# Hash-masked attention with a fused MLP: the first weight pieces loaded in another order, and a new written-out order of all instructions

## The chip, the cores and the metric

The kernel runs on one core of a Trainium2 chip. The metric is the device time of one execution in microseconds (us), taken as the median of a few runs. Beside these runs, one execution was recorded by the hardware profiler; all durations below come from that record.

A core has a matrix engine (PE, with its weight loads PEld), a vector engine (DVE), an activation engine (ACT), a general engine (POOL) and a synchronising engine (SP). Each executes its own queue strictly in the order in which it was given. Transfers are issued by SP, ACT or POOL and carried out by 16 DMA engines.

## The reference

The inputs are `q`, `k`, `v` of shape (4 batches, 8 heads, 768 positions, 64), a projection of 64 by 6, a scale of 512, and two MLP weights of 512 by 2048 and 2048 by 512, all float32.

```
bits   = (x @ proj) > 0                    # 6 bits for each row of q and of k
mask   = bucket(q bits) == bucket(k bits)
scores = where(mask, q @ k.T / 8, -1e9)
attn   = softmax(scores) @ v               # per batch and head
x      = heads side by side                # (4, 768, 512)
xn     = (x - mean) / sqrt(var + 1e-6) * g_ln
out    = x + relu(xn @ w_ch1) @ w_ch2
```

## The kernel before

**Units and stages.** The output rows are cut into 12 units of 256 rows; unit `u` belongs to batch `u // 3`. A unit has two head groups `g` of four heads, and three key pieces `kp` of 256 keys, so attention is 72 steps `s`, with `u = s // 6`, `g = (s % 6) // 3`, `kp = s % 3`. The mask is not a select: the bits of q and k, as plus or minus one half, are multiplied on PE into the same PSUM accumulation as the scores, so that a mismatch makes the exponent very small.

**The steps by name.** The order text calls the steps by short words, `name.engine.arguments`, where the engine letter is `t` for PE, `v` for DVE, `a` for ACT, `p` for POOL and `s` for SP. Those that matter below:

| word | engine | what it does | line |
|---|---|---|---|
| `lx`, `LX.b.g.t` | SP (one on ACT) | load q (`t`=0) or k (`t`=1) of a head group, of batch 0 in pieces, of later batches whole | L373, L508 |
| `lv.b.hs.c` | SP | load v of four heads; batch 0 whole, later ones in four pieces | L465, L467 |
| `lw1.p.n`, `lw2.p.n` | POOL | load quarter `n` of the first or second MLP weight, float32 in HBM to bf16 in SBUF | L446, L457 |
| `tn`, `tu` | DVE | transpose 32 by 32 blocks of q or k, batch 0 and later batches | L304 |
| `ca`, `CA` | DVE, ACT or POOL | cast the transposed q or k to bf16, batch 0 and later ones | L311 to L315 |
| `ha`, `hc`, `sl`, `hm` | PE | projections for the bits (float32), in several layouts | L394, L405, L418, L526 |
| `bh`, `bc`, `bt`, `bi` | DVE (`bi` also ACT) | turn projections into bits, or copy them | L307, L428, L430 |
| `mw`, `mr` | SP | write the bits to DRAM, and read them back in the layout of PE | L544, L547 |
| `cv`, `su`, `sp`, `sq`, `sc` | several | v to bf16, and its sums | L473 to L502 |
| `S`, `E`, `A` | PE, ACT, PE | scores of a step, their exponent, product with v | L570, L576, L595 |
| `na`, `nb`, `nc`, `ag`, `rs`, `ce` | DVE (`rs` POOL) | normalise the attention, statistics, centre and scale the row | L608 to L636 |
| `ft`+`fc`, or `fl` | PE+ACT/DVE, or SP | transpose the row; unit 0 on PE, later units by a DMA transpose | L644, L648, L650, L639 |
| `wg.v.n` | DVE | multiply quarter `n` of the first weight by the scale | L454 |
| `F`, `R` | PE, ACT or DVE | first MLP product of a unit in eight pairs of columns, and its relu | L657, L665, L667 |
| `D`, `Z` | PE, DVE | second product of unit 0, and its addition | L672, L675 |
| `sw`, `ss`, `P`, `Y` | DVE, DVE, PE, DVE | second product of units 1 to 11 by seven products instead of eight | L697, L708, L723, L728 |
| `O` | SP or ACT | store the output | L740, L742 |

**What sets the order.** The order is written out. `ORDER` is a text of 1185 words that a loop runs through, and every engine gets its part of the instructions in just that sequence. A step that waits holds back all that stands behind it in the same queue, on SP and POOL too. The buffers are written out as well: `SLOTS` says for each buffer pool which buffer each new tile takes.

```
    with tc.manual_schedule():
        for word in ORDER.split():
            name, eng, *args = word.split(".")
            OPS[name](ENGINES[eng], *map(int, args))
```

A later load of q or k reuses the buffer of an earlier one. Before the four loads of batch 1, POOL writes one element into the buffer (`gx`, L505), which waits until the transposes have read the old contents. SP's transfers take turns on eight semaphores: a transfer is issued only when the eighth one before it has landed.

**The start.** Nothing can run on PE until q and k of batch 0 have come in pieces, been transposed on DVE, projected and turned into bits. Then steps 0 to 5 run, and with them the attention of unit 0, while DVE transposes q and k of batch 1. Unit 0's first MLP product `F.0.3` needs the row of unit 0 and the weight quarter 1, scaled by `wg.v.1`. From there on attention steps and MLP products of earlier units alternate on PE until the end.

Of the kernel before, what the change touches and what calls it, by code (L numbers as in the profile page):

```python
# [22 lines left out]
E.a.1.1 bh.v.1.0.0 E.a.2.0 tn.v.0.0.1 ha.t.1.1.0 A.t.1.2 ca.p.1.1.0 sq.t.0.0 A.t.0.2 E.a.2.1
ca.v.1.0.0 S.t.4.2 bh.v.1.1.0 E.a.4.0 E.a.4.1 tn.v.1.1.2 sc.v.0.0 A.t.2.2 ca.p.1.1.2 ca.v.0.0.1
na.v.0.0 ha.t.1.1.2 bh.v.1.1.2 S.t.3.2 nb.v.0.0 E.a.3.1 E.a.3.0 hc.t.0.0.1 bc.v.0.0.1 tn.v.1.0.1
gx.p.1.0.1 sl.t.0.0.1 cv.p.0.4.2 tn.v.1.0.2 S.t.5.2 E.a.5.0 cv.v.0.4.0 E.a.5.1 bi.v.0.0.1 gx.p.1.1.0
hc.t.1.0.1 lw1.p.3 lg.s LX.s.1.0.0 tu.v.1.0.0.3 tu.v.1.0.0.2 S.t.8.2 E.a.8.1 sq.t.0.4 LX.s.1.0.1
E.a.8.0 bc.v.1.0.1 sl.t.1.0.1 A.t.4.2 lw1.p.1 tu.v.1.0.0.0 tn.v.0.0.2 lw1.p.2 tu.v.1.0.1.3 sc.v.0.4
A.t.5.2 lw1.p.0 tu.v.1.0.1.2 A.t.3.2 na.v.0.1 lw2.p.0 bi.a.1.0.1 S.t.6.2 tu.v.1.0.0.1 hc.t.1.0.2
bc.v.1.0.2 lw2.p.3 ca.a.1.0.1 nc.v.0.0 gx.p.1.1.1 LX.s.1.1.1 E.a.6.0 hc.t.0.0.2 E.a.6.1 bc.v.0.0.2  # L30
lv.s.1.4.1 sl.t.1.0.2 lv.s.1.4.2 lw2.p.2 S.t.7.2 E.a.7.1 sl.t.0.0.2 nb.v.0.1 lv.s.1.4.0 bi.v.0.0.2
bi.v.1.0.2 gt.t tu.v.1.0.1.1 tu.v.1.0.1.0 nc.v.0.1 ag.v.0.0 ag.v.0.1 S.t.9.2 E.a.7.0 E.a.9.1
gc.v ce.v.0.1 LX.s.1.1.0 hm.t.1.0 lv.s.1.0.0 lv.s.1.0.1 S.t.10.2 ce.v.0.0 ft.t.0.0 bt.v.1.0
ft.t.0.1 wg.v.1 mw.s.1.0 E.a.9.0 fc.v.0.1 A.t.6.2 lv.s.1.0.3 fc.a.0.0 lv.s.1.4.3 A.t.8.2
ca.a.0.0.2 A.t.7.2 wg.v.3 E.a.10.1 F.t.0.3 E.a.10.0 na.v.1.0 wg.v.2 S.t.11.2 E.a.11.0
R.v.0.3 F.t.0.4 R.v.0.4 nb.v.1.0 nc.v.1.0 F.t.0.7 E.a.11.1 S.t.14.2 lv.s.1.0.2 A.t.11.2
E.a.14.1 A.t.10.2 F.t.0.6 E.a.14.0 R.v.0.7 wg.v.0 A.t.9.2 CA.v.1.0.0 R.a.0.6 rs.p.0
S.t.12.2 mr.s.1.0.0 na.v.1.1 E.a.12.1 F.t.0.0 R.a.0.0 tu.v.1.1.0.3 F.t.0.1 R.v.0.1 mr.s.1.0.2
ca.v.1.0.2 mr.s.1.0.1 CA.p.1.0.1 E.a.12.0 nb.v.1.1 S.t.13.2 nc.v.1.1 ag.v.1.1 F.t.0.2 F.t.0.5
E.a.13.1 tu.v.1.1.1.0 R.a.0.2 S.t.16.2 D.t.0.0.0 E.a.13.0 A.t.13.2 ag.v.1.0 A.t.12.2 rs.p.1  # L40
tu.v.1.1.1.1 LX.s.2.0.1 tu.v.1.1.1.3 A.t.14.2 tu.v.1.1.0.0 tu.v.1.1.1.2 E.a.16.1 E.a.16.0 R.a.0.5 CA.a.1.1.1
na.v.2.0 D.t.0.0.1 tu.v.1.1.0.1 S.t.15.2 E.a.15.1 tu.v.1.1.0.2 hm.t.1.1 bt.v.1.1 S.t.17.2 D.t.0.1.0
E.a.15.0 D.t.0.1.1 nb.v.2.0 ce.v.1.0 A.t.16.2 mr.s.1.0.3 ce.v.1.1 A.t.15.2 E.a.17.0 E.a.17.1
A.t.17.2 su.p.1.0 cv.a.1.0.2 sw.v.3.1 na.v.2.1 nb.v.2.1 nc.v.2.1 CA.a.1.1.0 S.t.18.2 E.a.18.0
E.a.18.1 D.t.0.1.2 mw.s.1.1 D.t.0.1.3 Z.v.0.1 S.t.20.2 E.a.20.1 cv.v.1.0.0 fl.s.1.0 LX.s.2.0.0
E.a.20.0 nc.v.2.0 tu.v.2.0.0.2 D.t.0.0.2 D.t.0.0.3 S.t.19.2 Z.v.0.0 fl.s.1.1 ag.v.2.0 cv.a.1.4.0
ag.v.2.1 F.t.1.0 E.a.19.0 rs.p.2 tu.v.2.0.0.3 R.v.1.0 F.t.1.4 mr.s.1.1.0 A.t.18.2 tu.v.2.0.0.1
R.v.1.4 sw.v.2.1 sw.v.4.1 mr.s.1.1.2 ce.v.2.0 sw.v.3.0 F.t.1.2 sp.t.1.0 E.a.19.1 sw.v.2.0
mr.s.1.1.1 mr.s.1.1.3 S.t.21.2 sc.a.1.0 R.a.1.2 E.a.21.1 F.t.1.3 E.a.21.0 A.t.19.2 A.t.20.2
na.v.3.0 R.a.1.3 F.t.1.6 R.a.1.6 sw.v.4.0 S.t.22.2 LX.s.2.1.0 LX.s.3.0.1 sw.v.1.0 E.a.22.0  # L50
ce.v.2.1 fl.s.2.1 F.t.1.5 tu.v.2.0.0.0 R.v.1.5 E.a.22.1 F.t.1.7 nb.v.3.0 fl.s.2.0 R.a.1.7
S.t.23.2 E.a.23.1 P.t.1.2 Y.v.1.2 F.t.1.1 R.v.1.1 sw.v.1.1 S.t.24.2 E.a.23.0 lv.s.2.0.3
# [734 lines left out]
```

## Time and profile before

| | |
|---|---|
| median of 3 runs | 297.76 us (297.38 to 298.34) |
| the profiled execution, its own time | 298.12 us |
| its span, first to last instruction | 296.4 us |
| busy: PE, PEld | 286.4 us (97%), 227.6 us (77%) |
| busy: DVE, ACT, POOL | 210.8 us (71%), 202.9 us (68%), 57.1 us (19%) |
| mean granted PE clock | 0.993 |
| chain that ended last | PE 83%, DVE 7%, DMA 4%, issue 2% |
| transfers | 34.10 MB, mean 115 GB/s |

The profiled execution's time is 1.7 us longer than its span; that is work around the kernel. It lies 0.36 us above the median of the runs. PE is called busy in 97% of the span, but matmul ends are modelled and matmuls that wait in the middle of a group still count as busy, so the share hides stalls. They are found by the number of matmuls in a stretch, or by the time from one step's start to the next.

### The profile page before, as it was taken

The numbers are of one execution on the slowest core, as the hardware profiler recorded it, in microseconds if no ns is written. First come the engines' busy times: TensorE is split into PE (matmuls) and PEld (weight loads), VectorE is DVE, ScalarE is ACT, GpSimd is POOL, SyncE is SP. The second block draws the span as 40 slices with busy tenths as digits, with TensorE's granted clock in tenths as the row PEclk, the third lists the DMA queues.
The fourth block names the chain that finished last, engine by engine and source line by source line (L and its number), as shares of the span: only waits on it lengthen the run. The fifth ranks groups of instructions, "written<-read, shape, count | busy, mean of one in ns | idle before, by whom it ended". The sixth has DMA issues, their size and how long they took to land.

```text
span 296.4 us, 10520 instructions
## 1 busy us (share of the span) xinstructions
PE 286.4 (97%) x4646; PEld 227.6 (77%) x4650; DVE 210.8 (71%) x479; ACT 202.9 (68%) x227; POOL 57.1 (19%) x92
## 2 busy tenths in 40 slices
...
GB/s 216 313 336 159 278 291 240 162 160 222 38 189 65 201 157 13 216 115 2 30 102 143 63 154 29 55 62 2 73 39 2 71 22 2 108 0 108 0 91 72
DMA packets 31055, 34.10 MB, mean 115 GB/s; under 512 B 15521, under 2 KB 27809, under 8 KB 31010
## 3 DMA queue, kind: packets, MB, share of 16 engines
q1 hardware_dynamic: 25938, 28.72, 35.5%
...
## 4 chain that ended last, share of the span: by engine, by line
PE 83%; DVE 7%; DMA 4%; issue 2%; SPq 1%; ACT 1%; DVEq 0%; ACTq 0%
PE f L657 24%; PE sc L570 16%; PE X L723 12%; PE acc L595 10%; PE Yb L723 7%; PE Ya L723 3%; DMA xnT<-xc 3%; PE hf L394 3%; PE f L672 2%; PE hp L526 2%; ACT E L576 1%; DVE xc L630 1%; PE warm L363 1%; DMA out_dram<-x 1%; DVE hb L667 1%
## 5 line engine op out<-in xcount | busy, mean ns | idle before, releaser
L576 ACT ACTIVATE E<-sc,bias_sb 128x1024 bf16<-128x1024 f32 x144 | 153.3, 1112 | 44.8 <-PE sc L570 42.8
L657 PE MATMUL f<-xnT,w_sb 128*128 128x256 bf16 x768 | 93.4, 273 | 1.0 <-DMA xnT<-xc 1.0
L657 PEld LDWEIGHTS <-w_sb 128*128 128x128 bf16 x768 | 71.6, 98 | 14.0 <-issue 4.4
L665 ACT ACTIVATE hb<-f 128x512 bf16<-128x512 f32 x60 | 35.7, 596 | 32.5 <-PE f L657 32.4
L570 PE MATMUL sc<-qb,kb 32*128 32x256 bf16 x1152 | 53.1, 268 | 0.0
L570 PE MATMUL sc<-G 6*128 6x256 bf16 (+1 forms) x576 | 42.7, 273 | 1.3 <-DVE y L608 0.6
L595 PEld LDWEIGHTS <-E 128*128 128x128 bf16 x1152 | 40.7, 98 | 4.1 <-issue 2.5
L595 PE MATMUL acc<-vaug,E 128*128 128x65 bf16 x1152 | 43.5, 194 | 0.0
L723 PEld LDWEIGHTS <-hb 128*128 128x128 bf16 x352 | 32.9, 98 | 6.9 <-issue 3.1
L667 DVE TENSOR_SCALAR hb<-f 128x512 bf16<-128x512 f32 x36 | 24.5, 681 | 15.5 <-PE f L657 15.3
L635 POOL TENSOR_SCALAR rs<-mv 128x2 f32<-128x2 f32 x12 | 3.2, 270 | 160.5 <-DVE mv L624 155.5
L570 PEld LDWEIGHTS <-kb 32*128 32x128 bf16 x1152 | 30.8, 93 | 1.7
L728 DVE TENSOR_TENSOR x<-X,x 128x256 f32<-128x256 f32 x44 | 18.3, 418 | 18.5 <-PE X L723 18.2
L570 PEld LDWEIGHTS <-G 6*128 6x128 bf16 (+1 forms) x576 | 15.8, 91 | 17.3 <-issue 15.2
L723 PEld LDWEIGHTS <-S 128*128 128x128 bf16 x264 | 24.9, 97 | 4.7 <-issue 1.3
L304 DVE STREAM_TRANSPOSE T<-X 128x384 f32<-128x384 f32 (+2 forms) x52 | 26.6, 536 | 0.0
L723 PE MATMUL Yb<-w_sb,S 128*128 128x256 bf16 x176 | 22.9, 273 | 0.0
L723 PE MATMUL X<-wt,hb 128*128 128x256 bf16 x168 | 21.8, 273 | 0.0
L608 DVE SCALAR_TENSOR_TENSOR y<-vsB,acc 128x520 f32<-128x520 f32 x24 | 16.4, 685 | 6.4 <-PE acc L595 6.2
L617 DVE TENSOR_TENSOR x<-y,rc 128x512 f32<-128x512 f32 x24 | 16.6, 692 | 2.4 <-issue 1.2
L621 DVE BATCH_NORM_STATS2 st<-x 128x6 f32<-128x256 f32 x48 | 17.8, 414 | 0.3
L728 DVE TENSOR_TENSOR x<-Yb,x 128x256 f32<-128x256 f32 x22 | 9.2, 419 | 8.6 <-PE Yb L723 8.5
...
## 6 DMA issues: line engine op xcount, KB each, us to landing
...
w_sb<-in_moe_w_ch_dram POOLq DMA_DIRECT2D x8, 512.0 KB, 16.1
...
```

What stands on the lines that cost most here:

```text
L304: nc.vector.transpose(d[:, j], s[:, j, kj0 : kj0 + n])
L570: nc.tensor.matmul(sc(s, i // 2)[:, i % 2, 256 * kk : 256 * kk + 256], lh, rh, start=(rep == 0), stop=(rep == 2), skip_group_check=True,)
L576: nc.scalar.activation(E(s)[:, heads(h)], sc(s, h), AF.Exp, scale=EXP_SCALE, bias=bias_sb)
L595: nc.tensor.matmul(acc[:, qt, (D + 1) * i : (D + 1) * (i + 1)], E(s)[:, i, 256 * kk + P * qt : 256 * kk + P * qt + P], vaug(u // 3)[:, 4 * ...
L608: nc.vector.scalar_tensor_tensor(yt(u, g), vs, EPS_ROW, made[f"acc{u}{g}"][:, :, :A], op0=AOP.mult, op1=AOP.add,)
L617: nc.vector.tensor_tensor(xo, a[:, :, :, 0:D], rc.to_broadcast([P, 2, 4, D]), op=AOP.mult)
L621: nc.vector.bn_stats(stats(u)[:, qt, g], xt(u)[:, qt, 256 * g : 256 * g + 256])
L657: nc.tensor.matmul(f1[:, n].rearrange("p (t x) -> p t x", t=2), w1_sb[:, dt, P * nt : P * nt + P], xnT(u)[:, :, dt], start=(dt == 0), stop ...
L665: nc.scalar.activation(hb(u)[:, 2 * p : 2 * p + 2], f1, AF.Relu)
L667: eng.tensor_scalar_max(hb(u)[:, 2 * p : 2 * p + 2], f1, 0.0)
L723: nc.tensor.matmul(f2, lh[:, n], rh[:, n], start=(first and n == 0), stop=(n == 7), skip_group_check=True)
L728: nc.vector.tensor_tensor(x, made[f"{prod(u, k)}{u}"], x, op=AOP.add)
```

## The change

The diff rewrites `ORDER` and `SLOTS`, and nothing else. Its first lines and one of the buffer lines:

```diff
-mem.v lp.a lx.a.0.1.0.1 tab.a pf.v lx.s.0.0.0.1 warm.t wm.t.0 wm.t.1 wm.t.2
-wm.t.3 sel.p tn.v.0.0.0 p32.p tn.v.0.1.0 ca.p.0.1.0 lx.s.0.1.1.3 ha.t.0.0.0 wm.t.4 lx.s.1.1.0.3
+lp.a lx.a.0.1.0.1 lx.s.0.0.0.1 lx.s.0.1.1.3 lx.s.1.1.0.3 lx.s.1.0.0.1 lv.s.0.0.4 lx.s.0.0.1.3 lv.s.0.4.4 lx.s.1.0.1.3
+lg.s on.p.0 mem.v tab.a pf.v warm.t wm.t.0 wm.t.1 wm.t.2 wm.t.3
+sel.p tn.v.0.0.0 p32.p tn.v.0.1.0 on.p.1 lw1.p.3 ca.a.0.0.0 ha.t.0.1.0 wm.t.6 ha.t.0.0.0
...
-    X="0123023102132001",
+    X="0123021302312012",
```

 Both orders have the same 1185 steps. What differs is the sequence, the engine of some steps, and the buffers.

*The weights.* Before, the only weight piece among the first loads was quarter 1 of the second weight (`lw2.p.1`), and the other seven followed in one row. Now it is quarter 3 of the first weight (`lw1.p.3`), and the other three quarters of the first weight come next; the second weight's quarters stand further back. POOL's queue, all steps up to the last weight piece:

```
before: sel p32 ca.0.1.0 lw2.1 ca.0.1.1 ca.1.1.1 on.0 gx.1.0.0 pmem on.1 cv.0.0.2 cv.0.0.0 ca.1.1.0 ca.1.1.2 gx.1.0.1
        cv.0.4.2 gx.1.1.0 lw1.3 lw1.1 lw1.2 lw1.0 lw2.0 lw2.3 gx.1.1.1 lw2.2 rs.0 CA.1.0.1 rs.1 ...
after:  on.0 sel p32 on.1 lw1.3 ca.0.1.0 ca.0.1.1 ca.0.1.2 gx.1.0.0 cv.0.0.0 gx.1.0.1 ca.1.1.2 gx.1.1.1 cv.0.4.0 cv.0.4.2
        gx.1.1.0 lw1.1 lw1.2 lw1.0 pmem rs.0 lw2.1 lw2.0 CA.1.0.1 lw2.3 rs.1 lw2.2 ...
```

*SP's queue.* The first nine loads are unchanged. After them:

```
before: LX.1.0.0 LX.1.0.1 LX.1.1.1 lv.1.4.1 lv.1.4.2 lv.1.4.0 LX.1.1.0 lv.1.0.0 lv.1.0.1 mw.1.0 lv.1.0.3 lv.1.4.3 lv.1.0.2
        mr.1.0.0 mr.1.0.2 mr.1.0.1 LX.2.0.1 mr.1.0.3 mw.1.1 fl.1.0 LX.2.0.0 fl.1.1 mr.1.1.0 mr.1.1.2 mr.1.1.1 mr.1.1.3 ...
after:  LX.1.0.0 LX.1.0.1 mw.1.0 LX.1.1.0 mr.1.0.1 LX.1.1.1 lv.1.0.2 mr.1.0.2 lv.1.0.3 mr.1.0.3 mr.1.0.0 mw.1.1 lv.1.0.0
        lv.1.4.1 fl.1.1 lv.1.0.1 mr.1.1.2 mr.1.1.1 mr.1.1.0 fl.1.0 mr.1.1.3 lv.1.4.3 lv.1.4.2 LX.2.0.1 lv.1.4.0 ...
```

*DVE's queue in the start*, from the first transposes to the centred row of unit 0:

```
before: tn.0.0.0 tn.0.1.0 bh.0.0.0 tn.0.1.1 bh.0.1.0 tn.0.1.2 tn.1.1.1 bh.0.1.1 bh.1.1.1 tn.1.1.0 tn.1.0.0 bh.0.1.2 bh.1.0.0
        tn.0.0.1 ca.1.0.0 bh.1.1.0 tn.1.1.2 sc.0.0 ca.0.0.1 na.0.0 bh.1.1.2 nb.0.0 bc.0.0.1 tn.1.0.1 tn.1.0.2 cv.0.4.0 bi.0.0.1
        tu x2 bc.1.0.1 tu tn.0.0.2 tu sc.0.4 tu na.0.1 tu bc.1.0.2 nc.0.0 bc.0.0.2 nb.0.1 bi.0.0.2 bi.1.0.2 tu x2 nc.0.1 ag x2
        gc ce.0.1 ce.0.0
after:  tn.0.0.0 tn.0.1.0 bh.0.1.0 tn.0.1.1 bh.0.0.0 bh.0.1.1 tn.0.1.2 tn.1.1.0 bh.0.1.2 tn.1.1.1 tn.1.0.0 ca.1.1.0 bh.1.1.1
        ca.1.0.0 ca.1.1.1 bh.1.0.0 tn.1.1.2 cv.0.0.2 tn.0.0.2 bh.1.1.0 sc.0.0 tn.0.0.1 na.0.0 nb.0.0 bh.1.1.2 bc.0.0.1 tn.1.0.2
        bi.0.0.1 tn.1.0.1 sc.0.4 tu bc.1.0.2 tu x2 bc.1.0.1 tu x3 na.0.1 bc.0.0.2 nb.0.1 tu x2 nc.0.1 bi.0.0.2 nc.0.0 ag x2
        ce.0.0 ce.0.1 (gc follows)
```

*Engines.* Of the relus, 21 go from DVE to ACT and 17 the other way (64 on ACT instead of 60). Of the casts of q and k of later batches, ACT has 2 instead of 6, DVE 7 instead of 4, POOL 3 instead of 2. In the start, `ca.0.0.1`, `bi.1.0.2` and `fc.0.1` go from DVE to ACT, `ca.1.1.0` and `ca.1.1.1` from POOL to DVE, and `ca.0.1.2` from ACT to POOL.

*PE's queue.* From the first MLP product on, it holds the same groups at nearly the same places; for example, from unit 1's second product:

```
before: F.1.7 S.23 P.1.2 F.1.1 S.24 P.1.1 F.2.1 A.23 S.26 A.22 P.1.5 ...
after:  S.23 F.1.7 F.1.1 S.24 F.2.1 A.22 P.1.2 A.23 S.26 P.1.1 P.1.5 ...
```

More of the change, by code (lines that the diff above doesn't have):

```diff
@@ L23 @@
[L23 to L52, printed above, removed]
@@ new lines @@
+E.a.4.0 E.a.4.1 gx.p.1.0.1 tn.v.0.0.2 ca.a.0.0.2 bh.v.1.1.0 A.t.2.2 sq.t.0.0 LX.s.1.0.1 sc.v.0.0
+A.t.1.2 A.t.0.2 ca.p.1.1.2 tn.v.0.0.1 ca.a.0.0.1 gx.p.1.1.1 S.t.3.2 ha.t.1.1.2 E.a.3.0 cv.p.0.4.0
+na.v.0.0 hc.t.0.0.1 nb.v.0.0 E.a.3.1 bh.v.1.1.2 bc.v.0.0.1 S.t.5.2 E.a.5.1 sl.t.0.0.1 tn.v.1.0.2
+bi.v.0.0.1 cv.p.0.4.2 sq.t.0.4 tn.v.1.0.1 E.a.5.0 sc.v.0.4 hc.t.1.0.2 S.t.8.2 E.a.8.0 gx.p.1.1.0
+tu.v.1.0.0.2 bc.v.1.0.2 hc.t.1.0.1 lw1.p.1 tu.v.1.0.0.3 A.t.4.2 tu.v.1.0.0.0 A.t.3.2 E.a.8.1 bc.v.1.0.1
+lw1.p.2 sl.t.1.0.1 bi.a.1.0.1 A.t.5.2 tu.v.1.0.0.1 tu.v.1.0.1.2 lw1.p.0 sl.t.1.0.2 bi.a.1.0.2 ca.a.1.0.1
@@ new lines @@
+tu.v.1.0.1.0 S.t.6.2 E.a.6.0 E.a.6.1 na.v.0.1 hc.t.0.0.2 bc.v.0.0.2 sl.t.0.0.2 nb.v.0.1 tu.v.1.0.1.1
+tu.v.1.0.1.3 S.t.7.2 hm.t.1.0 E.a.7.0 S.t.9.2 nc.v.0.1 bi.v.0.0.2 nc.v.0.0 ag.v.0.0 ag.v.0.1
+ce.v.0.0 ce.v.0.1 pmem.p rs.p.0 gt.t E.a.7.1 A.t.7.2 A.t.6.2 A.t.8.2 bt.v.1.0
+gc.v E.a.9.0 E.a.9.1 ft.t.0.1 fc.a.0.1 wg.v.1 ft.t.0.0 fc.a.0.0 lw2.p.1 S.t.10.2
+E.a.10.0 E.a.10.1 na.v.1.0 F.t.0.3 wg.v.3 wg.v.2 R.a.0.3 S.t.11.2 F.t.0.7 E.a.11.0
+mw.s.1.0 F.t.0.4 R.v.0.7 LX.s.1.1.0 R.v.0.4 S.t.14.2 F.t.0.6 E.a.11.1 A.t.9.2 E.a.14.1
@@ new lines @@
+nb.v.1.0 nc.v.1.0 E.a.14.0 mr.s.1.0.1 A.t.11.2 A.t.10.2 wg.v.0 LX.s.1.1.1 lv.s.1.0.2 mr.s.1.0.2
+lw2.p.0 S.t.12.2 R.a.0.6 na.v.1.1 lv.s.1.0.3 nb.v.1.1 E.a.12.1 CA.p.1.0.1 tu.v.1.1.0.2 mr.s.1.0.3
+nc.v.1.1 CA.v.1.0.0 ag.v.1.0 E.a.12.0 F.t.0.1 R.a.0.1 F.t.0.0 S.t.13.2 ag.v.1.1 E.a.13.1
+E.a.13.0 lw2.p.3 mr.s.1.0.0 A.t.14.2 A.t.12.2 R.v.0.0 F.t.0.5 F.t.0.2 rs.p.1 tu.v.1.1.0.0
+tu.v.1.1.1.0 tu.v.1.1.0.1 ce.v.1.1 A.t.13.2 na.v.2.0 ca.a.1.0.2 nb.v.2.0 lw2.p.2 S.t.16.2 R.a.0.2
+R.a.0.5 E.a.16.1 D.t.0.0.0 D.t.0.0.1 tu.v.1.1.0.3 E.a.16.0 tu.v.1.1.1.3 tu.v.1.1.1.1 tu.v.1.1.1.2 CA.p.1.1.1
@@ new lines @@
+CA.a.2.1.0 F.t.3.1 R.v.3.1 mr.s.2.1.2 mr.s.2.1.1 E.a.38.0 F.t.3.3 R.v.3.3 mr.s.2.1.0 A.t.33.2
+na.v.5.1 E.a.38.1 tu.v.3.0.0.0 F.t.3.5 R.a.3.5 F.t.3.2 R.a.3.2 S.t.36.2 E.a.36.0 P.t.3.1
+ss.v.3.1 ss.v.3.2 P.t.3.2 Y.v.3.2 S.t.39.2 O.s.2.1 E.a.36.1 ss.v.3.4 P.t.3.5 E.a.39.0
+cv.p.2.0.2 A.t.36.2 LX.s.3.0.1 Y.v.3.1 P.t.3.6 Y.v.3.5 P.t.3.3 O.s.2.3 E.a.39.1 S.t.40.2
+E.a.40.0 E.a.40.1 ss.v.3.3 Y.v.3.6 Y.v.3.3 P.t.3.7 fl.s.4.0 nb.v.5.1 fl.s.4.1 tu.v.3.0.1.0
+F.t.4.3 Y.v.3.7 tu.v.3.0.0.2 P.t.3.4 Y.v.3.4 O.s.3.0 on.p.3 A.t.37.2 nc.v.5.1 ag.v.5.0
@@ new lines @@
+ag.v.7.0 P.t.5.5 E.a.52.0 mr.s.3.1.3 na.v.8.0 S.t.53.2 E.a.53.1 Y.v.5.5 P.t.5.3 Y.v.5.1
+nb.v.8.0 P.t.5.6 ss.v.5.3 mr.s.3.0.1 E.a.53.0 Y.v.5.6 mr.s.3.1.0 Y.v.5.3 S.t.54.2 CA.v.3.1.0
+P.t.5.7 E.a.54.0 F.t.6.0 R.a.6.0 A.t.53.2 Y.v.5.7 ag.v.7.1 P.t.5.4 E.a.54.1 rs.p.7
+F.t.6.6 Y.v.5.4 O.s.5.1 O.s.5.2 F.t.6.3 R.a.6.3 S.t.55.2 mr.s.3.1.2 R.v.6.6 A.t.52.2
+A.t.51.2 na.v.8.1 E.a.55.1 E.a.55.0 F.t.6.4 ce.v.7.0 S.t.56.2 R.a.6.4 ce.v.7.1 su.p.3.0
+F.t.6.5 E.a.56.1 F.t.6.2 R.a.6.5 E.a.56.0 S.t.58.2 R.v.6.2 E.a.58.1 fl.s.7.0 P.t.6.2
@@ new lines @@
+nc.v.8.0 Y.v.6.2 ss.v.6.1 ss.v.6.2 P.t.6.1 E.a.58.0 Y.v.6.1 cv.p.3.0.2 A.t.56.2 nb.v.8.1
+ss.v.6.3 sp.t.3.0 sc.a.3.0 nc.v.8.1 A.t.55.2 S.t.57.2 E.a.57.1 fl.s.7.1 F.t.7.5 R.a.7.5
+A.t.54.2 cv.a.3.4.0 na.v.9.0 P.t.6.6 Y.v.6.6 ss.v.6.4 E.a.57.0 P.t.6.5 Y.v.6.5 ag.v.8.0
+S.t.59.2 P.t.6.7 ag.v.8.1 Y.v.6.7 P.t.6.3 Y.v.6.3 rs.p.8 E.a.59.0 E.a.59.1 S.t.60.2
+E.a.60.1 E.a.60.0 O.s.5.3 F.t.7.0 O.s.5.0 cv.p.3.4.2 A.t.58.2 P.t.6.4 Y.v.6.4 R.a.7.0
+A.t.57.2 S.t.61.2 E.a.61.0 O.s.6.1 E.a.61.1 su.p.3.4 sp.t.3.4 ce.v.8.1 fl.s.8.1 ce.v.8.0
@@ new lines @@
+sc.v.3.4 F.t.7.4 F.t.7.6 R.a.7.6 A.t.59.2 nb.v.9.0 O.s.6.3 S.t.64.2 E.a.64.0 E.a.64.1
+F.t.7.2 na.v.9.1 R.v.7.4 R.v.7.2 F.t.7.7 S.t.62.2 E.a.62.1 F.t.7.3 E.a.62.0 nb.v.9.1
+R.v.7.7 F.t.7.1 R.v.7.3 R.a.7.1 S.t.63.2 A.t.62.2 P.t.7.1 A.t.61.2 nc.v.9.1 nc.v.9.0
+ag.v.9.1 ss.v.7.1 O.s.6.2 E.a.63.1 ss.v.7.2 P.t.7.2 ss.v.7.3 E.a.63.0 Y.v.7.2 Y.v.7.1
+A.t.60.2 na.v.10.0 S.t.65.2 P.t.7.6 Y.v.7.6 P.t.7.5 ss.v.7.4 E.a.65.0 ag.v.9.0 rs.p.9
+P.t.7.7 Y.v.7.5 Y.v.7.7 S.t.68.2 E.a.68.0 ce.v.9.1 P.t.7.3 Y.v.7.3 P.t.7.4 O.s.6.0
```

175 lines of the change are left out of this document (81 added, 94 removed).

## The prediction

> **What bounds the kernel now.** I first read busy shares: PE leads with 97%. That share can't be the bound as it stands, so I counted. Step to step, undisturbed, PE needs 0.77 us for a scores step `S`, 0.49 for `A`, 0.87 for an `F`, `P` or `D`, 1.44 for an `hm` (the chain of waits has these pieces). 72 S, 72 A, 180 F, P and D, and 6 hm make 55 + 35 + 157 + 9 = 256 us; the projections, sums and warm-up of the start add 20 and the first matmul starts at 1.1. That is 277 us in either order, as both hold the same PE steps. The last matmul ends at 292.1, so PE loses 15 us; 4.3 more are the last stores. Set beside the order, the loss lies so: 2.9 us until 27 us, 2.9 more until the first MLP product at 39.2, 0.9 from there to 68, 1.8 from 68 to 89, and 6.4 over the last 200 us, a few tens of nanoseconds at a time but for two waits. So the start is the stage to read. By windows (length, then busy time and count of each engine, clock, DMA share, GB/s):
>
> ```profile
> core 0: us, PE busy (x) PEld busy (x) DVE busy (x) ACT busy (x) POOL busy (x), PEclk, DMA share, GB/s
> 10.00:15.00 5.00, 4.99 (x63) 3.18 (x61) 3.56 (x10) 5.00 (x5) 3.64 (x11) 1.00 1.14 298
> 15.00:20.00 5.00, 5.00 (x87) 3.99 (x89) 3.34 (x8) 3.58 (x5) 1.94 (x4) 1.00 1.09 377
> 20.00:25.00 5.00, 3.46 (x91) 2.19 (x94) 4.83 (x14) 3.87 (x5) 2.15 (x4) 1.00 0.52 203
> 25.00:30.00 5.00, 4.88 (x142) 4.10 (x142) 4.69 (x13) 4.78 (x6) 4.07 (x7) 1.00 1.04 159
> 30.00:35.00 5.00, 4.42 (x76) 3.03 (x77) 4.65 (x15) 4.23 (x5) 0.97 (x2) 0.79 1.15 287
> 35.00:40.00 5.00, 5.00 (x112) 3.76 (x104) 3.38 (x11) 3.44 (x6) 1.78 (x2) 0.87 1.15 293
> ```
>
> From 20 to 35, DVE is full and PE isn't; before 20 DVE has 3.1 us idle in ten. DVE's timeline, with its idle time in brackets, says why:
>
> ```profile
> 16.66 0.77 DVE L304 STREAM_TRANSPOSE tp<-X 128x256 f32<-128x256 f32 x2 [1.92 <-DMA X<-in_q_dram]
> 17.36 0.38 DVE L313 TENSOR_SCALAR qb<-tp 128x512 bf16<-128x512 f32 x1
> ...
> 18.99 1.23 DVE L313 TENSOR_SCALAR qb<-tp 128x512 bf16<-128x512 f32 x1
> ...
> 33.89 0.88 DVE L628 TENSOR_SCALAR xc<-x,mv 128x512 bf16<-128x512 f32 x2
> 36.62 0.56 DVE L307 TENSOR_SCALAR B<-hp 128x384 bf16<-128x384 f32 x1 [1.84 <-PE hp L526]
> ```
>
> DVE stands at `tn.0.0.1` until its q has landed, with work queued behind that needs no q. From there to `ce` at 34.77 it runs nearly without a gap, and PE waits for its bits (`gt`, `hm`). And PE's clock was halved in the middle of it:
>
> ```profile
> 33.00:34.00 1.00, 1.00 (x15) 0.46 (x12) 0.99 (x6) 0.23 (x1) 0.05 (x1) 0.50 1.10 371
> 34.00:35.00 1.00, 1.00 (x16) 0.63 (x19) 0.78 (x2) 1.00 (x1) 0.92 (x2) 0.50 1.05 290
> 35.00:36.00 1.00, 1.00 (x20) 0.62 (x16) 0.00 (x0) 1.00 (x2) 1.00 (x2) 0.50 1.14 263
> ```
>
> There `hm.1.0` took 2.60 instead of 1.44, and `bt.1.0` on DVE waited for it with `wg.1` behind it.
>
> **The change, part by part.** *Weights.* Before, the quarters of the first weight, issued from 23.78 on, landed at 29.2, 32.6, 38.6 and 44.9, and the `wg` that use them started at 37.1 to 45.0: none was waited for, so loading them earlier gains nothing by itself. But `wg.0` started just as its quarter came, so a start shortened by 3 us needs it earlier. Now three instead of four pieces follow at about 24, with SP's loads of batch 1 out of the way until 34; at the first two pieces' pace (3.4 us each) the last is there at about 36. Cost nothing.
>
> *The early piece.* `lw1.3` is issued at about 4.3 (POOL's rows in sequence) instead of `lw2.1` at 6.94; same size. Its sharing with the first loads comes some 2.7 us earlier: while `lw2.1` moved 299 KB in 12.5 to 15, SP's queue moved 337 KB, against 750 to 924 in the windows before. So k of group 1 (9.7) and v (13.1) may land 1 to 2 us later, but the q at 16.57 behind both doesn't, as the bytes before it are the same. DVE's step at 16.6 keeps its time.
>
> *DVE in the start.* Out of the stretch 16.66 to 34.77 go `tn.1.1.2` (0.76), `ca.1.0.0` (0.38) and a `cv` (0.52), which now stand ahead of the wait, and `ca.0.0.1` (1.23) and `bi.1.0.2` (0.38), now on ACT: 3.3 us. Into the 2.95 us that DVE was idle from 9.8 to 16.66 come the first three, and two casts of k that POOL did. A k cast of this shape on DVE is not in the trace; the q casts beside it took 0.38, and 1.23 beside a POOL copy. I take 0.55, between, nearer to the undisturbed row: 0.76 + 0.38 + 0.52 + 1.1 = 2.8, which fits. At 1.23 each it would be 4.1, and 1.2 are given back. `bt` now stands behind `ce`, and `hm` comes sooner: the 1.84 goes too. By DVE, F.0.3 could start over 3 us earlier.
>
> *ACT is late next.* From the first exponent at 9.89 it has ten steps of 2.12 until unit 0 is transposed, two q casts (0.64 each), two `bi` (0.37) and another (0.65), and two `fc` (0.58): 25.2 us, and about 1 of waiting for the first scores, so F.0.3 at 36 instead of 39.2. Allowing 0.5 for waits between the queues, the start gains **2.7** (1.5 if the k casts are dear or the clock halves again over 1.2 us; 3.7 if neither engine waits).
>
> *From 39 to 68.* DVE's rows give 15.0 us of work in 12.6 of PE's between F.0.3 and `D.0.0.0`, before 14.4; rows overlap by about a tenth. So it stays just covered, the gain is kept, and 0.3 is lost at worst. Weight quarters of w2 now stand behind `rs.0` and `rs.1` on POOL, which wait for statistics: quarters 1, 0 and 3 are issued at about 34 to 37, and at 5 us each beside other loads are there by 40 to 50, for D at 49; quarter 2 at 47, there by 55, for D at 58. Covered by 4 us; every microsecond beyond would be a stall of PE.
>
> *SP.* `mw.1.0` now stands ahead of `LX.1.1.0` and `LX.1.1.1`: SP waits for `bt.1.0`, about 33.7, and behind it wait these two loads, `lv` and `mr`; for them `tu.1.1`, `hm.1.1`. They landed at 42.8 and 36.2; now I get 40 and 47 at 160 and 120 KB per us (SP's queue beside weights, 35 to 50). `tu.1.1.1` comes at about 47.5 in DVE's queue. No stall, with nothing to spare. `lv.1.0.1` stands behind `mw.1.1` and `fl.1.1`, lands at about 60; ACT needs it at 61 (`cv.1.0.2`). Both margins cost 0.3 together.
>
> *Later.* Two waits are read from PE's timeline:
>
> ```profile
> 79.09 1.03 PE L723 MATMUL Ya<-w_sb,hb 128*128 128x256 bf16 x8 [1.05 <-DVE hb L667]
> 109.27 1.03 PE L657 MATMUL f<-xnT,w_sb 128*128 128x256 bf16 x8 [0.55 <-DMA xnT<-xc]
> ```
>
> The first is `P.1.2`, waiting for `R.1.5`, which stood behind four `sw` (0.67 to 1.71). Now 6.4 us of PE steps lie between the starts of `F.1.5` and `P.1.2`, before 2.5, and three more `sw` are done before unit 1's products begin: 0.8 gone. For the transposed rows I compared `ce` to the first `F` in PE time: 4.4 for unit 3 (before 3.8), 4.9 for unit 5 (4.9), 4.7 to 7.1 for units 6, 9, 10 and 11 (before 2.6 to 6.4): 0.3 gained. New tight spots: `P.2.2` has 0.49 us for a relu of 0.68 on DVE. Steps with under 1.5 us of PE work between a producer and its user through ACT or DVE are 94, before 94: no other difference to price, and 0.3 lost.
>
> *Sum.* On the profiled execution's own 298.12: minus 2.7, 0.8, 0.3, plus 0.3, 0.3, 0.3 gives 295.2. That execution is 0.36 above the median, so the forecast is **294.9**.
>
> **The rivals.** (1) *The start gains only about 1*: k casts at 1.23 on DVE (1.2) and DVE full after 39 (0.3). For it speaks that DVE is at 1.0 of PE's time there; against it, that 0.38 is what such casts took undisturbed. 296.6. (2) *The early piece delays the first loads*: if the q at 16.57 slips by the 1 to 2 us that the ones before it do, the head's chain starts later and what DVE saves goes: 297.3. Against it: equal bytes by then. The Trainium skill ("DMA: Bandwidth & Descriptors", Queues, rings and completion order) says the DMA engines serve queues in turn, packet by packet, which speaks against putting a weight beside first loads; the 337 beside 299 KB agree. (3) *Slower: the loads behind `mw.1.0`*. If the weights leave SP's queue 80 KB per us, as in 47.5 to 50, `LX.1.1.1` lands at 52 to 54 instead of 47. `tu.1.1.1` then holds DVE, and behind it `na.2.0`, which frees the accumulator that `S` needs. Every microsecond past 47.5 costs one, past 50.6 the kernel is slower; at 53 it is 5.5 lost against 2.9 gained, and if about 1 of it falls on waits that are there anyway, 1.5 more than now: 299.3. (4) *The change doesn't reach the end*: steps merely swap stalls, 297.8.
>
> **How the numbers follow.** Forecast 0.48, (1) 0.12, (2) 0.08, (3) 0.26, (4) 0.06. A difference within 0.3%, 0.9 us, can't be told from none. Faster: forecast and (1), 0.60; same: (2), (4), 0.14; slower 0.26. The likeliest case's own range is 293.9 to 296.1 (start 3.7 to 1.5, the later terms kept). For 8 in 10 I reach down to 292.9, where none of the three losses of 0.3 comes, and up to 299.0, which leaves out the worse half of (3).
>
> **What would show it.** Right: F.0.3 starts at 35.5 to 37.5; DVE has under 1 us idle from 12 to 16.6; `bt.1.0` no longer waits 1.8; `P.1.2` comes without a wait. Wrong: DVE waits for X at about 48, ACT for vn at 61, PE for w_sb, or PE's clock halves again and F.0.3 starts after 38; or new gaps between 100 and 290 of over 1 us.

## The result, and the profile after

The changed kernel takes 295.31 us (median of 12 runs, 293.81 to 297.24) against 298.01 for the kernel before in the same set (12 runs). The ratio is 0.9904, with a 95% interval of 0.988 to 0.9928. A second set on another occasion gave 0.9876 (0.9853 to 0.99). So it is faster, by 2.7 us in the first set; 294.9 was forecast. The profiled execution took 294.45, which is 0.86 below its median, with a span of 292.7 and a granted clock of 0.999. So the two profiles differ by 1.0 us more than the medians do.

The windows of the start, with the same columns as in the prediction:

```profile
core 0: us, PE busy (x) PEld busy (x) DVE busy (x) ACT busy (x) POOL busy (x), PEclk, DMA share, GB/s
10.00:15.00 5.00, 5.00 (x62) 3.44 (x63) 4.30 (x12) 4.85 (x5) 1.14 (x3) 1.00 1.12 317
15.00:20.00 5.00, 5.00 (x109) 4.00 (x108) 4.35 (x12) 4.41 (x6) 2.26 (x4) 1.00 1.08 385
20.00:25.00 5.00, 4.46 (x110) 3.08 (x110) 4.62 (x13) 4.35 (x6) 2.90 (x5) 1.00 0.52 211
25.00:30.00 5.00, 4.61 (x144) 3.73 (x136) 4.77 (x12) 5.00 (x8) 1.78 (x4) 1.00 0.97 148
30.00:35.00 5.00, 5.00 (x124) 4.33 (x120) 4.96 (x14) 4.27 (x5) 2.73 (x4) 1.00 1.14 196
35.00:40.00 5.00, 4.39 (x71) 2.93 (x71) 5.00 (x13) 4.92 (x7) 2.31 (x3) 1.00 0.97 244
```

DVE works 8.65 us between 10 and 20, where it had 6.90, and PE gets through 109 matmuls instead of 87 from 15 to 20. The clock stays at 1.00. From 30 to 35 the DMA engines carry 196 GB/s instead of 287: SP's loads are still held behind `mw.1.0`. DVE's timeline shows the empty place ahead of the late q filled, and a new loss:

```profile
15.32 0.48 DVE L307 TENSOR_SCALAR G<-hf,hrow 128x256 bf16<-128x256 f32 x1 [0.63 <-PE hf L394]
15.72 0.76 DVE L304 STREAM_TRANSPOSE tp<-X 128x256 f32<-128x256 f32 x2
16.40 0.52 DVE L475 CAST vaug<-vn 128x768 bf16<-128x768 f32 x1
16.84 0.76 DVE L304 STREAM_TRANSPOSE tp<-X 128x256 f32<-128x256 f32 x2
...
32.79 0.55 DVE L307 TENSOR_SCALAR B<-hp 128x384 bf16<-128x384 f32 x1
...
33.44 3.55 DVE L454 TENSOR_SCALAR w_sb<-w_sb,gT 128x512 bf16<-128x512 bf16 x4
```

`tn.0.0.1` at 16.84 comes without its wait of 1.92, and `bt.1.0` at 32.79 without its 1.84. But the four steps of `wg.1` take 3.55, where all `wg` of before took 1.13 each. Two of them last 1.55 instead of 0.34, beside this on POOL:

```profile
33.42 1.60 POOL L457 DMA_DIRECT2D w_sb<-in_moe_w_ch_dram  x2
35.00 1.58 POOL L315 CAST kb<-T 128x1536 bf16<-128x1536 f32 x1
```

On PE, `F.0.3` starts at 35.97 instead of 39.17 but stops after two matmuls for `wg.1`; and a wait of 1.24 stands ahead of `F.2.1`, in place of the one ahead of `P.1.2` (here at 79.94):

```profile
35.97 0.38 PE L657 MATMUL f<-xnT,w_sb 128*128 128x256 bf16 x2 [0.17 <-ACT xnT L648]
...
36.79 0.98 PE L657 MATMUL f<-xnT,w_sb 128*128 128x256 bf16 x6 [0.44 <-DVE w_sb L454]
...
78.57 1.05 PE L657 MATMUL f<-xnT,w_sb 128*128 128x256 bf16 x8 [1.24 <-DMA xnT<-xc]
...
106.30 1.04 PE L657 MATMUL f<-xnT,w_sb 128*128 128x256 bf16 x8
```

The last line is `F.3.6`, now without the wait for its transposed row. For comparison, `wg.1` and `F.0.3` in the profile of before:

```profile
37.10 1.13 DVE L454 TENSOR_SCALAR w_sb<-w_sb,gT 128x512 bf16<-128x512 bf16 x4
39.17 1.03 PE L657 MATMUL f<-xnT,w_sb 128*128 128x256 bf16 x8
```

### The profile page after: what moved, and what is told of

Its sections match the earlier page's. It is cut to its first block, busy times and chain, and to the rows that moved or that the text cites. A ratio compares the mean times of both kernels' runs of the same rounds, so it can differ in the third digit from the quotient of the medians.

```text
span 292.7 us, 10520 instructions
## 1 busy us (share of the span) xinstructions
PE 284.5 (97%) x4650; PEld 227.0 (78%) x4650; DVE 211.8 (72%) x475; ACT 199.8 (68%) x229; POOL 59.5 (20%) x94
## 4 chain that ended last, share of the span: by engine, by line
PE 92%; DVE 4%; DMA 2%; issue 0%
PE f L657 28%; PE sc L570 18%; PE X L723 13%; PE acc L595 12%; PE Yb L723 7%; PE Ya L723 3%; PE f L672 3%; PE hp L526 2%; DMA xnT<-xc 2%; PE hf L394 2%; PE warm L363 1%; DVE w_sb L454 1%; PE warm L366 1%; DVE x L617 1%; PE vp L494 0%; DVE st L621 0%
## 5 line engine op out<-in xcount | busy, mean ns | idle before, releaser
L576 ACT ACTIVATE E<-sc,bias_sb 128x1024 bf16<-128x1024 f32 x144 | 153.3, 1111 | 38.2 <-PE sc L570 35.5
L665 ACT ACTIVATE hb<-f 128x512 bf16<-128x512 f32 x64 | 37.9, 597 | 36.6 <-PE f L657 36.3
L570 PE MATMUL sc<-qb,kb 32*128 32x256 bf16 x1152 | 52.2, 267 | 0.0
L570 PE MATMUL sc<-G 6*128 6x256 bf16 (+1 forms) x576 | 41.5, 273 | 0.6 <-DVE G L307 0.5
L667 DVE TENSOR_SCALAR hb<-f 128x512 bf16<-128x512 f32 x32 | 21.8, 681 | 16.3 <-PE f L657 16.0
L570 PEld LDWEIGHTS <-kb 32*128 32x128 bf16 x1152 | 30.2, 93 | 1.6
L570 PEld LDWEIGHTS <-G 6*128 6x128 bf16 (+1 forms) x576 | 15.2, 91 | 16.2 <-issue 13.5
L304 DVE STREAM_TRANSPOSE T<-X 128x384 f32<-128x384 f32 (+2 forms) x52 | 26.3, 539 | 0.0
L617 DVE TENSOR_TENSOR x<-y,rc 128x512 f32<-128x512 f32 x24 | 17.5, 731 | 0.8
L480 POOL TENSOR_TENSOR t<-vn 128x768 f32<-128x768 f32 x6 | 10.9, 1818 | 20.0 <-DMA vn<-in_v_dram 20.0
```

The lines of the kernel that those rows point to most:

```text
L304: nc.vector.transpose(d[:, j], s[:, j, kj0 : kj0 + n])
L570: nc.tensor.matmul(sc(s, i // 2)[:, i % 2, 256 * kk : 256 * kk + 256], lh, rh, start=(rep == 0), stop=(rep == 2), skip_group_check=True,)
L576: nc.scalar.activation(E(s)[:, heads(h)], sc(s, h), AF.Exp, scale=EXP_SCALE, bias=bias_sb)
L617: nc.vector.tensor_tensor(xo, a[:, :, :, 0:D], rc.to_broadcast([P, 2, 4, D]), op=AOP.mult)
L665: nc.scalar.activation(hb(u)[:, 2 * p : 2 * p + 2], f1, AF.Relu)
L667: eng.tensor_scalar_max(hb(u)[:, 2 * p : 2 * p + 2], f1, 0.0)
```

## The experiments

All edits are to the order text; a word keeps its buffers unless something else is said. Ratios are to the kernel before, run on the same chip.

**Two joints, h1 and h2.** The first asks whether the start carries the gain, the second whether the rest does.

```
h1: words of after up to F.t.0.3, then the remaining words in the order of before
h2: words of before up to F.t.0.3, then the remaining words in the order of after
```

As built, 187 words stand ahead of `F.0.3` in h1: 173 of after, then 14 that stand there in before, among them SP's loads of batch 1 and three pieces of the second weight on POOL.

> The first 187 words are those of after (up to the first MLP product F.0.3), all that follows keeps the order of before. Theory (the start carries the gain): F.0.3 starts at 35.5 to 36.5 as in after, and what came later in after (one wait removed, another new, two waits for transposed rows gone) sums to about -1; so 298.0 - 2.5 = 295.5, between 295.0 and 296.2. Rival (the later order carries it): F.0.3 comes early but the 3 us are given back at waits that stand there anyway; 297 or more. The four pieces of the second weight stand here one behind the other on POOL beside wg.1: if writing descriptors on POOL holds DVE, wg.1 takes over 2 us as in after (3.55); if the POOL cast did it, wg.1 takes 1.13 to 1.3.

> The mirror: the first 187 words are those of before, what follows F.0.3 is ordered as in after. Theory: F.0.3 starts at about 39 as in before, the waits for transposed rows at F.3.6 and F.5.2 (0.7 and 0.65) are gone, and the wait ahead of F.2.1 is there instead of the one ahead of P.1.2; 297.0, between 296.5 and 298.0. Rival (the later order carries the gain): 295.5 to 296. Both gains should add up to that of after, 2.7, within 0.5, if the stages are independent.

h1 took 301.07, ratio 1.0076 (1.0044 to 1.0109); h2 301.81, ratio 1.01 (1.0068 to 1.0133). Both are slower than either kernel, so neither theory was met. I had given tiles the buffer whose last reader stands furthest back in the text. That isn't the buffer that is free first in time, and in h1 `hm.1.0` came only at 32.99 (after: 29.79), so its start wasn't that of after. They decide nothing on the question. In h1b below, with the same order and other buffers, `hm.1.0` starts at 29.46, so the buffers alone moved it by 3.5. On the side question h1 answers a part: with four descriptor writings beside `wg.1` and no cast, it took 1.72.

**The wait put back, e3.**

```
-... ca.v.1.0.0 ha.t.1.1.0 ca.v.1.1.1 ... tn.v.1.1.2 cv.v.0.0.2 ... tn.v.0.0.2 ... tn.v.0.0.1
+... ha.t.1.1.0 tn.v.0.0.1 ca.v.1.0.0 ca.v.1.1.1 ... tn.v.1.1.2 cv.v.0.0.2 ... tn.v.0.0.2
```

> After, with the transpose of the q that lands at 16.5 put back ahead of ca.1.0.0, ca.1.1.1, tn.1.1.2, cv.0.0.2 and tn.0.0.2 on DVE. Theory (what stands ahead of the wait makes DVE's stretch shorter): DVE idles 2 to 4 us ahead of 16.5 again, F.0.3 starts 1.5 to 2.5 later, time 1 to 2 longer: 296.3 to 297.3. Rival (DVE does not set the start, ACT or PE does): F.0.3 within 0.5 of 36.0, time 295.0 to 295.8.

298.37, ratio 0.9995 (0.9972 to 1.0018): the whole gain is gone. This kernel's text is 40 lines shorter, so L264 is L304 and L267 is L307. On DVE:

```profile
14.13 0.42 DVE L267 TENSOR_SCALAR G<-hf 128x256 bf16<-128x256 f32 x1
16.93 0.77 DVE L264 STREAM_TRANSPOSE tp<-X 128x256 f32<-128x256 f32 x2 [2.38 <-PE hf L354]
```

DVE stands for 2.38, and `S.4` on PE waits 2.1 for the bits behind it. The q had landed at 16.34; the last 0.5 of the wait is for PE, which until 16.89 read the buffer that this transpose writes. `F.0.3` starts at 40.24, 4.3 later than in after. PE's clock then fell to 0.66 in the window from 20 to 25, which is 1.7 us of PE's full speed; so by the trace at least some 2.5 of the 4.3 are not the clock's (an estimate). All twelve runs had a lower mean clock (0.988 to 0.994; after once in twelve), so the runs can't separate the two. DVE's placement is a necessary part, and the rival is out; how much more than the expected 1 to 2 us it costs by itself stays open.

**Casts back on DVE, e4.**

```
-ca.a.0.0.1  bi.a.1.0.2  fc.a.0.1
+ca.v.0.0.1  bi.v.1.0.2  fc.v.0.1
```

> After, with ca.0.0.1, bi.1.0.2 and fc.0.1 on DVE again instead of ACT. DVE has 1.3 to 2.2 us more to do before F.0.3, ACT 1.6 less. Theory (DVE still sets the start, ACT has slack): F.0.3 1 to 2 later, 296.3 to 297.0. Rival (ACT is late next, as the prediction has it): the exponents run ahead, F.0.3 within 0.5 of 36.0, 294.8 to 295.8.

296.03, ratio 0.9909 (0.9875 to 0.9944). That is after's time; a loss of 1 us isn't excluded. In its profiled execution `F.0.3` starts at 37.60, 1.6 later than in after, as the theory has it. That execution was the longest of its six (298.06; the others 295.13 to 296.36), with a clock of 0.994; but the clock was halved from 81.4 to 84.8, long behind `F.0.3`. So this one trace speaks for DVE and against ACT as what sets the start, and the times show no loss. That the move of these three steps to ACT brings anything is not shown.

**The weights undone, e1, and the weights alone, e2.**

```
e1, on after:   -lw1.p.3 (early) +lw2.p.1; +lw1.p.3 ahead of lw1.p.1; -lw2.p.1 (at 33)
e2, on before:  -lw2.p.1 (early) +lw1.p.3; -lw1.p.3 (at 24); +lw2.p.1 behind lw1.p.0
```

> After, with only the weight pieces back in the sequence of before: lw2.1 early beside the first loads, lw1.3 ahead of lw1.1, lw1.2, lw1.0 at about 24, and no lw2.1 at 33. Four quarters of the first weight then land by about 29, 33, 36 and 39 to 40 or later. Prediction's step (earlier weights gain nothing by themselves, but a start shortened by 3 us needs them): wg.2, wg.3 or wg.0 wait for 0 to 2 us, time 0 to 0.5 over after: 295.9 to 296.5 where after stands at 0.9904 of before. Rival A (the early quarter carries the gain): over 297.5. Rival B (lw2.1 leaves the stretch beside wg.1 and frees DVE by one blocked row of 1.55): up to 0.5 faster than after.

> Before, with only the weight pieces in the sequence of after: lw1.3 beside the first loads in place of lw2.1, and lw2.1 behind lw1.0. Prediction's step: no quarter was waited for in before, so within 0.3 of before (ratio 0.999 to 1.001). Rival (the weights carry the gain): ratio 0.991 to 0.995.

e2: 298.63, ratio 1.0 (0.9982 to 1.0017). e1: 294.89, ratio 0.9891 (0.9853 to 0.9929), the same as after. In e1 the quarters of the first weight landed at 29.4, 32.8, 35.3 and 38.9, and the last was multiplied at 42.34 without a wait. So the reordering of the weights, the part that gives the change its name, is worth nothing measurable in either kernel (the interval of e1 leaves 1.1 us to either side, that of e2 0.5). Even the shortened start doesn't need it.

**POOL cleared beside wg.1, e5.**

```
-... rs.p.0 ... lw2.p.1 ... lw2.p.0 ... CA.p.1.0.1 ... lw2.p.3
+lw1.p.0 lw2.p.1 lw2.p.0 lw2.p.3 ... CA.p.1.0.1 pmem.p rs.p.0
```

> After, with POOL's work beside wg.1 moved ahead: lw2.1, lw2.0 and lw2.3 are issued right behind lw1.0 (at 26.4 instead of 33.4 and 36.5), and the cast CA.1.0.1 (1.58) stands ahead of rs.0. Theory (a bf16 step of DVE waits until POOL's cast or descriptor writing ends): the four steps of wg.1 take 1.13 instead of 3.55, S.11 starts 0.9 earlier, time 0.5 to 1.0 less than after: ratio to before 0.987 to 0.9885. Rival A (the two rows of 1.55 are not POOL's doing): wg.1 stays over 3. Rival B (wg.1 shortens, but fc on ACT, or an exponent, holds F.0.3 at 36 anyway and later waits take the rest): wg.1 1.13 and a ratio of 0.990 as after.

294.75, ratio 0.9885 (0.9855 to 0.9916). In its timeline:

```profile
33.85 1.14 DVE L454 TENSOR_SCALAR w_sb<-w_sb,gT 128x512 bf16<-128x512 bf16 x4
```

`wg.1` takes 1.14 beside an idle POOL, so the 3.55 was POOL's doing. The next scores step, `S.11`, starts at 37.18 instead of 37.71, and the last product of all 0.3 earlier (287.09 instead of 287.39). Two profiled executions of after itself have `S.11` at 37.71 and 37.78, but the last product at 287.39 and 287.81. So the 0.5 at `S.11` is clear, and of the 0.3 at the end neither the traces nor the runs can tell.

**The transposed copies ahead of a load, e6.**

```
-... LX.s.2.0.0 fl.s.2.1 ... fl.s.2.0 ...
+... fl.s.2.1 ... fl.s.2.0 LX.s.2.0.0 ...          (and tu.v.2.0.0.1 behind tu.v.2.0.1.0)
```

> After, with the load LX.2.0.0 (768 KB) moved on SP behind the two transposed copies fl.2.1 and fl.2.0 of unit 2, and the DVE step tu.2.0.0.1 that needs it moved behind tu.2.0.1.0. Theory (the copies stand behind that load in the queue): they land by about 75.5 instead of 78.5, F.2.1 follows S.24 without its wait of 1.3, time 0.7 to 1.2 less: ratio 0.9865 to 0.988. Rival (the wait moves on to P.1.2, whose relu and sums on DVE end at about 79, as it was in before): F.2.1 without a wait, P.1.2 with one of about 1, ratio 0.990 as after.

294.14, ratio 0.9856 (0.9828 to 0.9885). On PE, `F.2.1` at 77.10 has no wait, nor has `P.1.2` at 78.47, but one stands at `P.1.4`:

```profile
77.10 1.05 PE L657 MATMUL f<-xnT,w_sb 128*128 128x256 bf16 x8
...
88.63 1.03 PE L723 MATMUL X<-wt,hb 128*128 128x256 bf16 x8 [1.14 <-DVE x L728]
```

DVE's and POOL's timelines say why:

```profile
86.15 2.09 DVE L697 TENSOR_TENSOR wt<-w_sb,wt 128x1024 bf16<-128x1024 bf16 x1
```

```profile
85.88 1.81 POOL L480 TENSOR_TENSOR t<-vn 128x768 f32<-128x768 f32 x1 [9.07 <-DMA vn<-in_v_dram]
```

`sw.4.0` takes 2.09 instead of 0.68, beside a sum on POOL. The copies' wait was the load's doing; the wait moved on as the rival says, only further back. In the traces 0.3 is left at the end, which is within what two executions of after differ by.

**After again, and two more.**

> The changed kernel itself, unaltered, so that the two others have it on the same chip. Ratio to before 0.990, between 0.988 and 0.993 as measured; the wait ahead of F.2.1 (1.3) and wg.1 beside POOL (3.55) are there again.

294.57, ratio 0.9876 (0.9853 to 0.99), just under what was expected. `wg.1` takes 3.55 again; the wait ahead of `F.2.1` is 1.58 here, 1.24 before.

```
h1b: as h1, with the buffers of after in the start and those of before behind it
e8:  e5 and e6 together, and sw.v.4.0 from behind Y.v.1.7 of the order to behind Y.v.1.1
```

> The first 187 words of after, then the order of before, as in h1, but with the buffers of after for the tiles of the start and those of before for the rest, instead of buffers picked by the place in the text. Theory (the start carries the gain, and h1 lost it by its buffers): ratio 0.990 to 0.994, F.0.3 at 36 to 37. Rival (the gain of the start is taken back at the waits that before has later, at P.1.2, F.3.6 and F.5.2): ratio 0.996 to 1.002 with F.0.3 at 36 to 37.

h1b took 301.2, ratio 1.0103 (1.0074 to 1.0133), with `F.0.3` at 41.3: neither the theory nor the rival. `hm.1.0` starts at 29.46, even before after's 29.79, so the start is there. Then this, on PE:

```profile
29.46 1.49 PE L526 MATMUL hp<-T,p 128*32 128x192 f32 x27
...
33.88 0.52 PE L526 MATMUL hp<-T,p 128*32 128x192 f32 x5 [2.93 <-issue]
```

PE stands still after matmul 27 of the 32, and "issue" means that the profile shows nothing it waited for. In the same trace a 16 KB packet of the queue of kind "instruction" ends at 32.35. The same packet in other traces:

| | packet ends | matmul 27 starts | matmul 28 starts | packet to 28 |
|---|---|---|---|---|
| before | 31.24 | 35.80 | 35.81 | 4.57 |
| after | 29.50 | 30.95 | 30.95 | 1.45 |
| e5 | 29.61 | 31.22 | 31.23 | 1.62 |
| e1 | 29.71 | 30.71 | 31.13 | 1.42 |
| h1b | 32.35 | 30.63 | 33.88 | 1.53 |

Where PE is early, matmul 28 comes about 1.5 after the packet's end, whatever the time; where PE is late, nothing is seen of it. After and e5 have no pause there, but no more distance either, so they seem to have next to no slack. What h1b has in common with before, and after has not, are SP's loads of batch 1 ahead of `mw.1.0`. Hence the last one:

**The loads ahead again, e7.**

```
-mw.s.1.0 LX.s.1.1.0 ... LX.s.1.1.1 ... lv.s.1.0.0 lv.s.1.4.1 ... lv.s.1.0.1 ... lv.s.1.4.2 lv.s.1.4.0
+LX.s.1.1.1 lv.s.1.4.1 lv.s.1.4.2 lv.s.1.4.0 LX.s.1.1.0 lv.s.1.0.0 lv.s.1.0.1 mw.s.1.0
```

> After, with SP's loads of the second half of batch 1 (LX.1.1.1, three lv.1.4, LX.1.1.0, two lv.1.0) put ahead of mw.1.0 again, in the order of before; all else as in after. They are then issued from 19.5 on instead of from 33.8. Theory (with the start 3 us earlier these loads and the weights fill the DMA engines while PE's next block of instructions is fetched; in h1b PE stood 2.93 within hm.1.0 with no releaser, its block arriving at 31.2 to 32.4 instead of 28.6 to 29.5, and the clock was halved behind it): PE stands 2 to 3.5 in or near hm.1.0, F.0.3 at 38.5 to 41.5, ratio 0.996 to 1.010. Rival (h1b lost it by something else that lies in the order behind F.0.3): F.0.3 at 36 to 36.5, PE without that gap, ratio 0.986 to 0.992. This also prices mw.1.0 ahead of the loads, which the prediction took for a risk only.

298.46, ratio 1.001 (0.9977 to 1.0043): by the median of the runs the whole gain is gone again, with DVE's order untouched. PE's timeline, and the windows:

```profile
29.80 1.49 PE L526 MATMUL hp<-T,p 128*32 128x192 f32 x27
33.40 0.52 PE L526 MATMUL hp<-T,p 128*32 128x192 f32 x5 [2.12 <-issue]
```

```profile
core 0: us, PE busy (x) PEld busy (x) DVE busy (x) ACT busy (x) POOL busy (x), PEclk, DMA share, GB/s
20.00:25.00 5.00, 4.84 (x119) 3.39 (x120) 4.60 (x13) 4.72 (x6) 2.87 (x5) 1.00 1.03 396
25.00:30.00 5.00, 4.37 (x129) 3.40 (x128) 4.46 (x12) 4.80 (x8) 1.45 (x4) 1.00 1.04 236
30.00:35.00 5.00, 2.88 (x61) 2.00 (x54) 3.42 (x11) 2.22 (x3) 2.75 (x5) 1.00 1.21 227
```

The DMA engines are full from 20 on (share 1.03, after 0.52). The packet starts at 30.8 instead of 28.6 and ends at 31.98; matmul 28 follows 1.42 later. PE itself had come equally far (`hm.1.0` at 29.80, after 29.79). `F.0.3` starts at 38.43, still 0.7 earlier than in before, and the last product 0.8 earlier. That the pause is the fetching of instructions is read from the packet and from the distance, which is 1.38 to 1.62 in all seven traces that have a pause there (e1, e4, e6, e7, e8, h1, h1b; in e3 it is 1.34, without a pause); that the loads cause the pause is shown by e7. The profiled execution had a clock of 1.00. The six runs of e7 with 0.996 or more have a median of 297.3, against 298.4 for the 13 such runs of before on the same chip. So about 1 us of the gain is left where the clock stays up, and the rest is lost in the six runs with a lower clock. And e7 is not SP's queue of before at the times of before: there these loads were issued from 28.4 on.

> After, with POOL cleared beside wg.1 as in e5, the load LX.2.0.0 behind the transposed copies as in e6, and sw.4.0 on DVE moved ahead by three sums of products, to where DVE waits for PE and POOL is idle. Theory (in e6 sw.4.0 took 2.09 instead of 0.68 beside a POOL sum and P.1.4 waited 1.2 for it): no wait at wg.1, F.2.1 or P.1.4; 0.3 + 1.2 to 1.5 less than after: ratio 0.985 to 0.9865. Rival (waits move on each time, as in e6): 0.988 to 0.990.

e8 took 293.60, ratio 0.9841 (0.9814 to 0.9868), against 294.57 and 0.9876 for after on the same chip. Its ratio is the lowest here. DVE and PE:

```profile
33.65 1.14 DVE L454 TENSOR_SCALAR w_sb<-w_sb,gT 128x512 bf16<-128x512 bf16 x4
...
82.53 0.68 DVE L697 TENSOR_TENSOR wt<-w_sb,wt 128x1024 bf16<-128x1024 bf16 x1
```

```profile
77.50 1.05 PE L657 MATMUL f<-xnT,w_sb 128*128 128x256 bf16 x8
...
87.83 1.05 PE L723 MATMUL X<-wt,hb 128*128 128x256 bf16 x8
```

All three waits are gone, and `P.1.4` starts 1.07 before after's 88.90. The intervals of e8 and after overlap, but both stand on the same runs of before, and four of e8's five runs are shorter than the shortest of after's five (294.16). So the 1.0 us between them is likely, from five runs each. How it divides among the three waits is not shown.

## Why the prediction was right, step by step

The sum said minus 3.8 on the profiled execution, and minus 2.9 with its three allowances for losses. The traces give 3.67 (298.12 to 294.45), or 2.7 by medians. By term, from PE's steps in the two profiles:

- *The start, minus 2.7.* It measures minus 3.2 at the first matmul of `F.0.3` (35.97, forecast 36) and minus 2.4 one scores step later. The size was right. Its reason was half of the truth: e3 shows that DVE's order is needed, e7 that it isn't enough.
- *DVE's pieces.* The casts of k took 0.61 and 0.64 on DVE (taken: 0.55). "ACT is late next" isn't borne out: with 1.6 us of ACT's work back on DVE (e4), `F.0.3` came 1.6 later in the one trace, where ACT as the limit would have left it at 36, and the times didn't change measurably. And PE's instructions arrive hardly earlier than PE needs them. The `cv` in the sum is two steps: `cv.0.4.0` left DVE for POOL, `cv.0.0.2` came from POOL; the amounts stay.
- *SP, plus 0.3.* This is the step that failed. `mw.1.0` ahead of the loads was priced as a risk alone. X landed at 39.3 and 46.6 (forecast 40 and 47) and nobody waited. `lv.1.0.1` landed at 63.0 (forecast 60), just as ACT came to need it. But the same edit kept the DMA engines free while PE's instructions came, and without it `F.0.3` gains 0.7 instead of 3.2 (e7). My third rival had its sign wrong: the loads behind `mw.1.0` are what lets the kernel be faster.
- *Weights, nothing.* Right, by e1 and e2. The last first-weight quarter landed at 35.5 (forecast 36), and `lw2.2` at 55.8 (55). But "a start shortened by 3 us needs it earlier" is not so in e1. And the prediction asked when the pieces land, not what issuing them does: on POOL from 33.4 on, they and the cast behind them held `wg.1`, which gave back 0.8 of the start.
- *P.1.2, minus 0.8.* It didn't come. `P.1.2` has no wait, but `F.2.1` just ahead of it got one of 1.24 for its transposed row, behind a load of 768 KB (e6): plus 0.2 in all.
- *Transposed rows, minus 0.3.* Mis-sized the other way: the waits at `F.3.6` and `F.5.2` are both gone, minus 1.4. That these two errors cancelled was luck.
- *The three losses of 0.3.* From 39 to 68 PE lost nothing more (`S.17` is 2.5 earlier than in before, as `S.11` is 2.4), and no new gap of over 1 us stands between 100 and 290.
- *The early piece.* v landed at 14.94 instead of 13.10, as forecast, and the q at 16.57 came at 16.44, which puts the second rival out. k of group 1 came at 9.26 instead of 9.71, not later; what came later beside v was the first piece of q of group 1, 11.85 instead of 10.43.
- *The halved clock* in the profile of before wasn't a property of its order. Of 19 runs of before in the first set of experiments, 13 had a clock of 0.998 or more and a median of 298.81; the other six had 299.08. It may have flattered the start all the same: h2 begins with the words of before, its clock stayed up there, and its `F.0.3` starts at 38.08 instead of 39.17. So up to 1.1 of the 3.2 may be the clock of that one execution; no trace of before with the clock up is at hand to decide it.
- *Slips in the working.* `F`, `P` and `D` are 181, not 180. ACT's list adds up to 25.0, not 25.2. The two terms of the first rival give 296.4, not 296.6. None moves the forecast by more than 0.2.
